# Batch 0 of a fused attention and two-block MLP kernel: strided heads first, mixing products as their inputs finish

## The chip, the cores and the metric

The kernel runs on one core of a Trainium2 chip. The metric is the time of one execution in microseconds (us): before the change the median of three runs is 950.33 us (949.88 to 951.0). A core has five engines that run at the same time and each take their instructions in a fixed order: TensorE (PE, matrix products; its weight loads are listed as PEld), VectorE (DVE), ScalarE (ACT), GpSimd (POOL) and SyncE (SP). Here SP only issues DMAs, and POOL mostly does.

## The reference

For 4 batches of 576 tokens, 8 heads of 64 compute attention, and two MLP blocks follow. Heads 0 to 3 see the last 32 tokens ("local"), heads 4 to 7 see every 32nd token ("strided").

```
scores = scale * np.matmul(q, k.transpose(0, 1, 3, 2))
mask_local = (rel >= 0) & (rel < stride)
mask_strided = (rel >= 0) & (pos[None, :] % stride == pos[:, None] % stride)
attn = softmax(where(mask_local if h < H // 2 else mask_strided, scores, -1e9))
x = (attn @ v), heads side by side            # [4, 576, 512]

h = xt @ U @ V                                # block 1: mixes tokens, U is 576x32, V is 32x576
u = x + h.transpose(0, 2, 1)
x = u + np.maximum(u @ w_ch1, 0.0) @ w_ch2    # 512 -> 2048 -> 512

mixed = np.real(fft(fft(x, axis=1), axis=2))  # block 2
u = x + mixed
un = (u - mu) / np.sqrt(var + 1e-06)
out = u + np.maximum(un @ w_ch1, 0.0) @ w_ch2
```

## The kernel before

The 2304 tokens lie in five chunks: four of 512 tokens, one for each batch (tile `ub0` to `ub3`), and one of 256 with what is left of all batches (`ur`). The MLP (`ffn`, L1109) goes chunk by chunk, in two halves of 1024 hidden units. A half is a first layer (L1140 to L1142, three matmuls for each product, since numbers are split into a high and a low 16-bit part), an eviction by ACT and DVE (L1146, L1147), and a second layer (L1172 to L1174). Of chunk 0 the first half's first layer is done for token tiles 0 and 1 first and then for 2 and 3, so it starts when two of the four tiles are ready.

Before the first MLP matmul stand the attention of batch 0 and the first weights. Attention is cut into nine units: `L00`, `L10`, `L01`, `L11` (local; head pair j, part u), `R` (the 64 left-over tokens, local) and `S00`, `S10`, `S01`, `S11` (strided). Each unit is a chain: scores on PE, a row maximum on DVE (L453), exponentials on ACT (L461), transposes on PE, a copy on ACT, the product with v on PE (L514, L557, L587), and the normalization on DVE (L466 to L473). Before the steps of a unit PE runs fillers (`warm`, L479), matmuls with no use; `WARM` says how many.

The strided units write their result in another token order to a tile `xs`. `unpermute` (L610) brings it into token order by a detour: SP stores `xs` to DRAM (`scr`) and loads it back into columns 256 to 511 of `ub0`. It is issued when the last of the four strided units is done. The token mixing takes two products: `mix_groups` (L623) splits each of six groups of the attention's output on ACT and DVE (L633, L634) and sums U's product into two PSUM banks `tb` (L637; groups 6, 8, 10 take `xs`, groups 0 and 2 `ub0`, group 4 `ur`); then `ts` is split (L672, L673), and V's product (L677) is added to `ub0` on DVE (L678), which needs the loaded-back columns. Then each tile is scaled, split, transposed on PE (L707) and copied (L711, L713), and is an operand of the MLP.

Weights come as 64-bit numbers in blocks of 128 rows (`raw`, 0.52 MB, four buffers; loads at L173). Of a block DVE makes 32-bit numbers (a cast at L147 and a shift at L150), and ACT sums the squares (L224). When eight blocks (a half) are through, one common scale follows (`w_scale`, L199), and each block is split (L166, L169). A buffer's next load waits for the shift.

Loads of batch 0 are issued by SP in the order of `LOADS` (L43; `r` left-over values, `l`, `s` queries and keys, `v`, `x` values, `m` the mixing matrices, `w` a weight block). Loads of batch 1 wait by `gate` (L390) for the first tile of `ub0` with V's product added.

Two lanes are written out by hand, side work (attention, later preparation) and weights. Until the first tiles are ready the string `STEPS` says which lane takes the next step; after that `TICKS`, one entry for each of 64 places inside chunks 0 and 1, and then the rates `RATES` by chunk, or `LATE` once the last FFT is done. PSUM banks come from pools with fixed counts (`bank`, L96).

## Time and profile before

| what | us |
|---|---|
| median of three runs | 950.33 (949.88 to 951.0) |
| the profiled execution | 948.61 |
| its span on the core | 946.8 |
| PE busy | 911.7 (96%) |
| DVE busy | 641.0 (68%) |
| ACT busy | 416.7 (44%) |

The profile is of one execution. Its span runs from the first to the last instruction; 1.81 us of its time lie around the span. Times in the rows are us from the start of the span. Busy time is the time in which an engine has an instruction running; for PE it does not tell useful matmuls from fillers, and a busy PE can be at half clock (the granted clock, 1.00 for 2.4 GHz and 0.50 for 1.2 GHz). A timeline row names a run of equal instructions; in brackets stands how long the engine stood idle just before it, and what ended that.

### The profile page before, as it was taken

What the parts mean: (1) busy time and instruction counts of PE and PEld (TensorE: products, weight loads), DVE (VectorE), ACT (ScalarE), POOL (GpSimd) and SP (SyncE); (2) the same over time, 40 slices, a digit from 0 to 9 for tenths busy, and PEclk for the clock granted to TensorE, in tenths of its full rate; (3) what the DMA queues carried; (4) which work ended last, traced back from release to release, by engine and by line L of the source; (5) the groups of instructions that cost most, each with busy time, mean ns of one, the idle gap of its engine ahead of it and who ended that gap; (6) DMA issues with size and microseconds to landing.
All of it is one profiled execution on the core that took longest, in us unless ns stands there. A gap on an engine that the chain in (4) does not pass through costs nothing.

```text
span 946.8 us, 15957 instructions
## 1 busy us (share of the span) xinstructions
PE 911.7 (96%) x6155; PEld 586.0 (62%) x6155; DVE 641.0 (68%) x1633; ACT 416.7 (44%) x996; POOL 47.9 (5%) x83
## 2 busy tenths in 40 slices
PE   8968999999999999999999989999999999999998
PEld 6747755555545664466456446555644588888897
DVE  2787967533343436642848966998699799865766
ACT  3865767423231433731537534342324264342433
POOL 1102100000000001100111300001000000000000
PEclk9958999999999999999999989999999999999999
DMA  9688761232201103501424400003010301212010
GB/s 316 219 268 263 261 238 50 63 101 96 66 20 27 40 12 115 174 1 33 120 91 158 120 14 2 0 7 83 1 39 7 79 7 34 41 52 34 2 46 24
DMA packets 64891, 78.62 MB, mean 83 GB/s; under 512 B 46512, under 2 KB 51760, under 8 KB 64816
## 3 DMA queue, kind: packets, MB, share of 16 engines
q1 hardware_dynamic: 59696, 44.49, 16.7%
q0 software_dynamic: 5120, 33.12, 10.4%
q8 instruction: 48, 0.79, 0.3%
q14 instruction: 27, 0.22, 0.1%
HBM read 60.16 MB, written 7.08 MB: 71 GB/s over the span
## 4 chain that ended last, share of the span: by engine, by line
PE 61%; DVE 17%; issue 9%; DMA 6%; ACT 4%; POOL 1%; SPq 1%; DVEq 0%; POOLq 0%; ACTq 0%
PE f L1140 7%; PE f L1141 7%; PE f L1142 7%; PE f L1172 7%; PE f L1173 7%; PE f L1174 7%; DMA raw<-in_w 3%; PE bk L1059 2%; PE bk L1057 2%; PE bk L1058 2%; DVE wslot L987 2%; DVE wslot L973 1%; DVE wslot L169 1%; DVE gl L981 1%; POOL raw L173 1%
## 5 line engine op out<-in xcount | busy, mean ns | idle before, releaser
L1140 PE MATMUL f<-ut,wslot 128*128 128x512 f16 (+1 forms) x480 | 170.7, 356 | 6.3 <-DVE gl L1147 5.6
L1141 PE MATMUL f<-ut,wslot 128*128 128x512 f16 (+1 forms) x480 | 169.9, 354 | 1.7 <-DMA ut<-lo 1.1
L1142 PE MATMUL f<-ut,wslot 128*128 128x512 f16 (+1 forms) x480 | 170.0, 354 | 0.0
L1172 PE MATMUL f<-wslot,gh 128*128 128x512 f16 x416 | 158.5, 381 | 0.8 <-DVE ub L1180 0.8
L1173 PE MATMUL f<-wslot,gh 128*128 128x512 f16 x416 | 158.2, 380 | 0.0
L1174 PE MATMUL f<-wslot,gl 128*128 128x512 f16 x416 | 158.2, 380 | 0.0
L1146 ACT ACTIVATE gh<-f 128x512 f16<-128x512 f32 (+1 forms) x120 | 64.3, 537 | 138.4 <-PE f L1142 137.9
L1147 DVE SCALAR_TENSOR_TENSOR gl<-f,gh 128x512 f16<-128x512 f32 (+1 forms) x120 | 73.8, 615 | 65.8 <-ACT gh L1146 64.6
L1141 PEld LDWEIGHTS <-wslot 128*128 128x128 f16 x480 | 47.6, 99 | 48.9 <-issue 11.2
L1140 PEld LDWEIGHTS <-wslot 128*128 128x128 f16 x480 | 47.8, 100 | 43.8 <-issue 4.8
L1142 PEld LDWEIGHTS <-wslot 128*128 128x128 f16 x480 | 47.5, 99 | 44.3 <-issue 2.1
L1174 PEld LDWEIGHTS <-gl 128*128 128x128 f16 x416 | 40.8, 98 | 49.2 <-issue 0.7
L1172 PEld LDWEIGHTS <-gh 128*128 128x128 f16 x416 | 41.4, 100 | 45.5 <-issue 0.5
L1173 PEld LDWEIGHTS <-gh 128*128 128x128 f16 x416 | 40.9, 98 | 44.8 <-issue 1.6
L1180 DVE SCALAR_TENSOR_TENSOR ub<-f,ivt,ub 128x512 f32<-128x512 f32 x48 | 35.6, 744 | 47.8 <-PE f L1174 47.7
L166 ACT ACTIVATE wslot<-wslot,wsc 128x512 f16<-128x512 f32 x64 | 46.0, 719 | 48.5 <-DVE wsc L230 23.3
L169 DVE SCALAR_TENSOR_TENSOR wslot<-wslot,wsc 128x512 f16<-128x512 f32 x64 | 47.8, 746 | 12.7 <-ACT wslot L166 11.9
L461 ACT ACTIVATE P<-bk,mx 108x64 f32<-108x64 f32 (+2 forms) x126 | 30.6, 331 | 45.8 <-DVE mx L456 36.5
L150 DVE SCALAR_TENSOR_TENSOR wslot<-raw,ztop 128x512 int32<-128x512 int32 x64 | 45.1, 713 | 3.6 <-ACT ztop L149 2.3
L224 ACT ACTIVATE wslot<-wslot 128x512 bf16<-128x512 f32 x64 | 40.1, 627 | 12.7 <-DVE wslot L150 7.8
L173 POOL DMA_DIRECT2D raw<-in_w x61 | 33.2, 544 | 246.1 <-DVE wslot L150 136.8
L453 DVE TENSOR_REDUCE mx<-bk 108x6 f32<-108x384 f32 (+4 forms) x44 | 19.8, 461 | 32.8 <-PE bk L496 19.2
(364 smaller groups left out, 1875.4 us busy)
## 6 DMA issues: line engine op xcount, KB each, us to landing
raw<-in_w POOLq DMA_DIRECT2D x61, 511.8 KB, 4.9
q<-in_ql SPq DMA_DIRECT2D x8, 576.0 KB
q<-in_qs SPq DMA_DIRECT2D x7, 594.0 KB
out<-ub SPq DMA_DIRECT2D x16, 256.0 KB
vl<-in_vl SPq DMA_DIRECT2D x8, 390.0 KB
vs<-in_vs SPq DMA_DIRECT2D x8, 390.0 KB
k<-in_kl SPq DMA_DIRECT2D x8, 320.0 KB
scr<-xs SPq DMA_DIRECT2D x8, 270.0 KB
```

What stands on the lines that cost most here:

```text
L150: V.scalar_tensor_tensor(out=i32(dst), in0=x, scalar=13, in1=zt, op0=ALU.logical_shift_right, op1=ALU.bitwise_or)
L166: A.activation(out=dst, in_=src, func=AF.Copy, scale=s)
L169: V.scalar_tensor_tensor(out=dst, in0=src, scalar=s, in1=hi, op0=ALU.mult, op1=ALU.subtract)
L173: (eng or G).dma_start(out=raw[:, 0:2047], in_=src[m].bitcast(U16)[:, 1:2048])
L1140: T.matmul(ps[:, 0:n], lhsT=wh, rhs=uh[:, k, cols], start=(k == 0), stop=False)
L1141: T.matmul(ps[:, 0:n], lhsT=wh, rhs=ul[:, k, cols], start=False, stop=False)
L1142: T.matmul(ps[:, 0:n], lhsT=wl, rhs=uh[:, k, cols], start=False, stop=(k == 3))
L1146: A.activation(out=gh[:, i, cols], in_=ps[:, 0:n], func=AF.Relu)
L1147: V.scalar_tensor_tensor(out=gl[:, i, cols], in0=ps[:, 0:n], scalar=0.0, in1=gh[:, i, cols], op0=ALU.max, op1=ALU.subtract)
L1172: T.matmul(ps, lhsT=ga, rhs=w[:, 0, :], start=(i == 0), stop=False)
L1173: T.matmul(ps, lhsT=ga, rhs=w[:, 1, :], start=False, stop=False)
L1174: T.matmul(ps, lhsT=gb, rhs=w[:, 0, :], start=False, stop=(i == HW - 1))
```

## The change

For batch 0 the strided units are put out first (`FIRST`), with their queries and keys in front in `qk` and their loads first in `LOADS`; `L01` and `L11` come after `R`. The mixing products no longer wait for all units: each of the six groups is put out when the units that it takes are done (`GNEED`), in the order of `MG0`, and the two `tb` banks are taken from the pool of four when the first group starts. The 24 fillers at the start become 28, the 75 others 57. `STEPS`, `TICKS`, `RATES` and `LATE` have new numbers. Batches 1 to 3 keep their order of units.

```diff
+GNEED = {0: ('L00', 'L10'), 2: ('L01', 'L11'), 4: ('R',), 6: ('S00', 'S10'), 8: ('S00', 'S10', 'S01', 'S11'), 10: ('S01', 'S11')}
...
-LOADS = ['r', 'l0', 'v0', 'v1', 'l1', 'm', 's0', 'w', 's1', 'x1', 'w', 'w', 'x0']
+LOADS = ['s0', 's1', 'x0', 'x1', 'm', 'l0', 'w', 'w', 'l1', 'v0', 'r', 'w', 'v1']
...
 MG = [[6, 0, 2], [8, 4, 10]]
...
-STEPS = 'ssssmmsssssmsssswswssswssssssswwwsswwwssssswswsswswsswssssswswswssssswswss'
...
+STEPS = 'ssmssssmsssmsssswssswsswsssssswsswwsssswwswswsswwssssssssswsssssssssswwswswwssw'
...
+FIRST = ['S00', 'S10', 'S01', 'S11', 'L00', 'L10', 'R', 'L01', 'L11']
+MG0 = [6, 8, 10, 0, 2, 4]
 ORDER = ['L00', 'L10', 'L01', 'L11', 'R', 'S00', 'S10', 'S01', 'S11']
...
             A.activation(out=ap, in_=late[0], func=AF.Copy)
...
     qk = []
-    QK = [(b, x, j) for b in range(NB) for x in "ls" for j in range(2)]
+    QK = [(b, x, j) for b in range(NB) for x in ("ls" if b else "sl") for j in range(2)]
...
     def qk_load():
         b, x, j = QK[len(qk)]
...
     def local_unit(b, j, u, q, k, v):
         Sb = bank()
-        if b == j == u == 0:
-            z = ones.bitcast(BF16)
-            warm(Sb[:, 0:256], WARM['i'], z[:, 0:128], z)
         nm = f'L{j}{u}'
         warm(Sb[:, 0:416], WARM[nm][0], idb, mL[1])
         n = LCOLS[u]
...
     def strided_unit(b, j, u, q, k, v, xs):
         Sb = bank()
+        if b == j == u == 0:
+            z = ones.bitcast(BF16)
+            warm(Sb[:, 0:256], WARM['i'], z[:, 0:128], z)
         nm = f'S{j}{u}'
         warm(Sb[:, 0:416], WARM[nm][0], idb, mL[1])
         msk = mS[u].rearrange("p (n w) -> p n w", n=1).to_broadcast([128, 3, 128]) if u else mS[u]
...
         xs = atp.tile([128, NT, 256], F32, tag="xs", bufs=1, name="xs")
         qk_upto(4 * b + 3)
         v = loaded if b == 0 else {n: VT[n[0]](b, int(n[1:] or 0)) for n in ("v0", "v1", "r", "x0", "x1")}
-        for u in ORDER:
+        l0, s0 = (4 * b, 4 * b + 2) if b else (2, 0)
+        for u in ORDER if b else FIRST:
             if u == "R":
-                yield u, rest_unit(b, qk[4 * b:4 * b + 2], v["r"]), xs
+                yield u, rest_unit(b, qk[l0:l0 + 2], v["r"]), xs
                 qk_upto(4 * b + (5 if b else 4))
                 continue
             j, i = int(u[1]), int(u[2])
             if u[0] == "L":
-                yield u, local_unit(b, j, i, *qk[4 * b + j], v[f"v{j}"]), xs
+                yield u, local_unit(b, j, i, *qk[l0 + j], v[f"v{j}"]), xs
             else:
-                yield u, strided_unit(b, j, i, *qk[4 * b + 2 + j], v[f"x{j}"], xs), xs
+                yield u, strided_unit(b, j, i, *qk[s0 + j], v[f"x{j}"], xs), xs
                 if i == 1 and b:
                     qk_upto(4 * b + 6 + j)
...
     def attention(b):
         live = []
         left = {u for u in ORDER if u[0] == "S"}
+        done = set()
+        rest = list(MG0) if b == 0 else []
         it = attn_units(b)
         more = True
         tb = None
...
                     live.append([u, nm])
                 except StopIteration:
                     more = False
-                    tb = [bank(), bank()]
-                    live.append([mix_groups(b, xs, tb, MG[0]), "M"])
+                    if b:
+                        tb = [bank(), bank()]
+                        live.append([mix_groups(b, xs, tb, MG[0]), "M"])
             for z in list(live):
                 try:
                     next(z[0])
                 except StopIteration:
                     live.remove(z)
                     left.discard(z[1])
+                    done.add(z[1])
+                    while rest and done.issuperset(GNEED[rest[0]]):
+                        if tb is None:
+                            tb = [pb.tile([128, 512], F32, tag="b", name="bk") for _ in range(2)]
+                        live.append([mix_groups(b, xs, tb, [rest.pop(0)]), "M"])
                     if z[1][0] == "S" and not left:
                         unpermute(b, xs)
                     continue
                 yield
-        yield from mix_groups(b, xs, tb, MG[1])
+        if b:
+            yield from mix_groups(b, xs, tb, MG[1])
         p0 = 32 * b
         ts = atp.tile([128, 512], F32R, tag="PT", bufs=PTB, name="ts")
         for x in (1, 0):
```

Three places show what moved. Line numbers in the rows of the change are 3 to 13 higher for the same instruction. First, DVE just ahead of the first MLP matmuls, before the change. `ut` with `xs`, `ub0` or `ur` is a mixing group's split (L634), `raw` and `wsc` rows are weight blocks, `ts` is the split before V's product.

```order
L150 SCALAR_TENSOR_TENSOR wslot_913<-raw_583,ztop1_87 128x512
L156 TENSOR_SCALAR wsc_97<-wsc_97 128x8
L634 TENSOR_TENSOR ut1_626<-xs_161,ut0_625 108x512
L158 TENSOR_SCALAR wsc_97<-wsc_97 128x8
L634 TENSOR_TENSOR ut1_626<-ub0_89,ut0_625 128x512
L147 CAST ztop0_86<-raw_611 128x512
L169 SCALAR_TENSOR_TENSOR wslot_396<-wslot_397,wsc_97,wslot_396 128x512
L634 TENSOR_TENSOR ut1_626<-xs_161,ut0_625 108x512
L634 TENSOR_TENSOR ut1_626<-ur_93,ut0_625 32x512
L169 SCALAR_TENSOR_TENSOR wslot_397<-wslot_412,wsc_97,wslot_397 128x512
L673 TENSOR_TENSOR ts_689<-bk_587,ts_689 32x256
L673 TENSOR_TENSOR ts_689<-bk_586,ts_689 32x256
```

Five of the six group splits stand here or just above, behind the last strided unit. With the change, DVE some 50 rows further up, where the last strided units end and the first local one begins (`mx` a row maximum, `rc` a reciprocal; L638 was L634):

```order
L638 TENSOR_TENSOR ut1_407<-xs_161,ut0_406 108x512
L470 RECIPROCAL rc_385<-rc_385 108x6
L150 CAST ztop0_86<-raw_147 128x512
L476 TENSOR_TENSOR xs_161<-bk_375,rc_385 108x3x128
L153 SCALAR_TENSOR_TENSOR wslot_432<-raw_147,ztop0_86 128x512
L638 TENSOR_TENSOR ut1_407<-xs_161,ut0_406 108x512
L456 TENSOR_REDUCE mx_425<-bk_414 128x4
L459 TENSOR_SCALAR mx_425<-mx_425 128x4
L638 TENSOR_TENSOR ut1_407<-xs_161,ut0_406 108x512
```

The three splits from `xs` have moved up here, between weight blocks and the local units. And with the change the rows ahead of the first MLP matmuls:

```order
L153 SCALAR_TENSOR_TENSOR wslot_886<-raw_577,ztop1_87 128x512
L159 TENSOR_SCALAR wsc_97<-wsc_97 128x8
L638 TENSOR_TENSOR ut1_407<-ub0_89,ut0_406 128x512
L161 TENSOR_SCALAR wsc_97<-wsc_97 128x8
L150 CAST ztop0_86<-raw_632 128x512
L150 CAST ztop1_87<-raw_638 128x512
L153 SCALAR_TENSOR_TENSOR wslot_920<-raw_632,ztop0_86 128x512
L172 SCALAR_TENSOR_TENSOR wslot_389<-wslot_390,wsc_97,wslot_389 128x512
L686 TENSOR_TENSOR ts_673<-bk_342,ts_673 32x256
L153 SCALAR_TENSOR_TENSOR wslot_948<-raw_638,ztop1_87 128x512
L172 SCALAR_TENSOR_TENSOR wslot_390<-wslot_432,wsc_97,wslot_390 128x512
L691 TENSOR_TENSOR ub0_89<-ub0_89,bk_682 128x512
```

One split (from `ub0`) and one half of `ts` are left at this place; the weight rows are as many as before. The second engine is SP, which issues DMAs in order: before the change, from the last loads of batch 0 to the first of batch 1 (`vs`, `vl` values, `scr` the detour).

```order
L427 DMA vs<-in_vs 128x780
L173 DMA raw<-in_w 128x2047 x2
L427 DMA vs<-in_vs 128x780
L421 DMA vl<-in_vl 32x2x65
L614 DMA scr_100<-xs 18x256 x2
L615 DMA scr_100<-xs 54x5x256 x2
L619 DMA ub_89<-scr_100 128x1x256 x2
L621 DMA ur<-scr_100 32x256
L619 DMA ub_89<-scr_100 128x1x256 x2
L621 DMA ur<-scr_100 32x256
L409 DMA q<-in_ql 128x1152
```

The small `vl` row is a load of batch 1 that went out ahead of the detour. With the change, the same stretch:

```order
L176 DMA raw<-in_w 128x2047
L423 DMA vl<-in_vl 96x1040
L424 DMA vl<-in_vl 32x2x65
L618 DMA scr_100<-xs 18x256
L619 DMA scr_100<-xs 54x5x256
L618 DMA scr_100<-xs 18x256
L619 DMA scr_100<-xs 54x5x256
L623 DMA ub_89<-scr_100 128x1x256 x2
L625 DMA ur<-scr_100 32x256
L424 DMA vl<-in_vl 32x2x65
L623 DMA ub_89<-scr_100 128x1x256 x2
L625 DMA ur<-scr_100 32x256
```

The detour follows the same loads, in four stores; the small `vl` load now stands between the two pairs of loads back into `ub0`, so that the second pair waits for what it waits for (the values of `L00` and `L01`, whose buffer it takes).

## Rows read from the trace of the kernel before

**Rows 1.** busy time of each engine over the whole page

```profile
PE 911.7 (96%) x6155; PEld 586.0 (62%) x6155; DVE 641.0 (68%) x1633; ACT 416.7 (44%) x996; POOL 47.9 (5%) x83
```

**Rows 2.** windows: busy us by engine (PE, PEld, DVE, ACT, POOL), clock, DMA share, GB/s

```profile
0.00:11.16 11.16, 8.74 (x46) 5.88 (x47) 0.17 (x1) 1.59 (x2) 2.96 (x9) 1.00 0.84 243
11.16:27.29 16.13, 16.05 (x145) 10.98 (x143) 9.26 (x34) 8.95 (x31) 0.00 (x0) 1.00 1.02 383
27.29:65.41 38.12, 28.38 (x205) 23.03 (x205) 30.35 (x80) 28.04 (x84) 6.03 (x11) 0.72 0.68 206
65.41:104.90 39.49, 36.16 (x333) 29.42 (x332) 31.47 (x94) 23.98 (x68) 6.44 (x12) 0.88 0.87 294
104.90:130.00 25.10, 24.56 (x177) 17.01 (x174) 20.48 (x51) 17.63 (x52) 4.96 (x9) 1.00 0.84 297
```

**Rows 3.** timeline of PE: start, us, line, what [idle before <-releaser]

```profile
10.03 1.10 PE L496 MATMUL bk<-k,q 128*128 128x96 f32 x8 [1.36 <-DMA q<-in_ql]
...
44.28 2.43 PE L557 MATMUL bk<-vs,PZ 128*108 128x65 f32 x12 [1.43 <-ACT PZ L547]
...
49.15 5.37 PE L637 MATMUL bk<-ut,US 108*128 108x256 f32 x16 [0.20 <-ACT ut L633]
55.44 1.22 PE L677 MATMUL bk<-ts,VS 128*128 128x512 f32 x2 [0.93 <-DVE ts L673]
62.38 0.61 PE L707 MATMUL bk<-idh,gh 128*128 128x128 f16 x4 [5.71 <-ACT gh L166]
...
65.52 0.74 PE L1140 MATMUL f<-ut,wslot 128*128 128x256 f16 x2
...
104.90 0.38 PE L1172 MATMUL f<-wslot,gh 128*128 128x512 f16 x1
```

**Rows 4.** timeline of DVE, the longest waits before the first FFN matmul

```profile
14.94 0.16 DVE L466 TENSOR_SCALAR rc<-bk 128x4 f32<-128x4 f32 x1 [3.01 <-PE bk L514]
...
18.73 0.56 DVE L453 TENSOR_REDUCE mx<-bk 128x4 f32<-128x384 f32 x1 [2.96 <-PE bk L496]
...
57.66 0.69 DVE L678 TENSOR_TENSOR ub<-ub,bk 128x512 f32<-128x512 f32 x1 [0.88 <-DMA ub<-scr]
59.00 0.69 DVE L678 TENSOR_TENSOR ub<-ub,bk 128x512 f32<-128x512 f32 x1 [0.66 <-DMA ub<-scr]
...
65.41 0.42 DVE L711 COPY ut<-bk 128x512 f16<-128x512 f16 x1
```

**Rows 5.** timeline of SP's DMA queue: the detour through DRAM

```profile
48.40 0.87 SPq L615 DMA_DIRECT2D scr<-xs  x2
53.45 1.24 SPq L619 DMA_DIRECT2D ub<-scr  x2
...
55.75 1.09 SPq L619 DMA_DIRECT2D ub<-scr  x2
```

**Rows 6.** groups of DVE instructions by form, 0 to 66 us

```profile
L150 DVE SCALAR_TENSOR_TENSOR wslot<-raw,ztop 128x512 int32<-128x512 int32 x12 | 8.1, 685 | 0.1
...
L634 DVE TENSOR_TENSOR ut<-xs,ut 108x512 fp32r<-108x512 f32 x3 | 2.1, 689 | 0.0
```

**Rows 7.** the weight loads of line L173, 0 to 140 us

```profile
DMA to landing us min/median/max: 3.7/5.1/9.7
```

**Rows 8.** timeline of PE, the same matmuls at two clocks

```profile
67.19 0.42 PE L1140 MATMUL f<-ut,wslot 128*128 128x256 f16 x1
67.41 0.42 PE L1141 MATMUL f<-ut,wslot 128*128 128x256 f16 x1
...
68.41 0.27 PE L1141 MATMUL f<-ut,wslot 128*128 128x256 f16 x1
68.51 0.27 PE L1142 MATMUL f<-ut,wslot 128*128 128x256 f16 x1
```

**Rows 9.** windows of the late part, columns as in rows 2

```profile
700.00:720.00 20.00, 18.71 (x87) 8.42 (x86) 20.00 (x54) 4.78 (x9) 0.00 (x0) 1.00 0.15 34
720.00:740.00 20.00, 20.00 (x94) 9.11 (x93) 19.70 (x73) 8.65 (x17) 0.00 (x0) 1.00 0.19 40
```

More of the change, by code (lines that the diff above doesn't have):

```diff
@@ L47 @@
 MG = [[6, 0, 2], [8, 4, 10]]
-TICKS = 'ws|wwsssww|wsswws|wwsw|wsws|swswwsw|w|swwswwssw|wsw|wsswwss|w|swsw|wwsww|wws|wwwsss|ssw|wwssws|wsssw|wswswsww|ss|ws|ssw|ssw|wss|swwsw|ww|swwss|wsw|wwsws|wws|ss|wwwwww|ww|www|wswwssw|wwsssss|wwww|w|ws|ww||w|ws|sssww|wswww|wwws|ws|wwss||sw|w|wwswwww||wssww|s|wwsw||ww||wwswwwws|sws|wwwwsww|ws|sws'
-STEPS = 'ssssmmsssssmsssswswssswssssssswwwsswwwssssswswsswswsswssssswswswssssswswss'
+TICKS = 'wws|wwwssw|swssw|sww|swssws|wwwsss||wwwss|wwws|wssswwwswww|s|wss|ww|sssw|swwsws|ww|sswswsww|wsswswws|wwsww|s|wwwwws|sws|ssww|ss|swsws|sw|wsswww|ssw|wwws|wsw|sw|wwws|s|wwww|sssws|swwwwwsswws|ww|w|s|wsww|www|ssw||wwsww|wsww|ws|wsww|wwswws||ss|wwsw|wwswww|s|wwwwss|w|ws|www|wswss|w|swswws|wwww|wwww|s|wwwsssw'
+STEPS = 'ssmssssmsssmsssswssswsswsssssswsswwsssswwswswsswwssssssssswsssssssssswwswswwssw'
 PTB = 2
-WARM = {'i': 24, 'L00': (1, 6, 3), 'L10': (5, 2, 2), 'L01': (6, 6, 1), 'L11': (5, 2, 4), 'R': (2, 6, 4), 'S00': (4, 5, 1), 'S10': (1, 3, 0), 'S01': (0, 3, 0), 'S11': (3, 3, 1)}
+WARM = {'i': 28, 'L00': (0, 3, 0), 'L10': (5, 0, 2), 'L01': (6, 3, 4), 'L11': (0, 6, 0), 'R': (1, 0, 6), 'S00': (0, 0, 6), 'S10': (6, 6, 0), 'S01': (3, 2, 1), 'S11': (0, 0, 3)}
+FIRST = ['S00', 'S10', 'S01', 'S11', 'L00', 'L10', 'R', 'L01', 'L11']
+MG0 = [6, 8, 10, 0, 2, 4]
 ORDER = ['L00', 'L10', 'L01', 'L11', 'R', 'S00', 'S10', 'S01', 'S11']
@@ L55 @@
 TP = (0, 1, 2, 3, 4, 5, 6, 7)
-LATE = [0.7999999999999999, 0.40000000000000013]
-RATES = [[3.5, 1.9], [3.5, 1.0], [3.0, 2.0], [4.25, 3.75], [1.5, 1.5], [1.05, 2.25], [1.0, 4.0], [2.0, 2.25], [4.25, 1.0], [1.9, 0.5]]
+LATE = [0.75, 0.7]
+RATES = [[2.5, 2.0], [2.5, 0.5], [2.0, 1.5], [5.0, 2.75], [1.5, 1.5], [1.05, 2.25], [1.0, 4.0], [3.45, 0.6999999999999998], [4.25, 2.0], [3.35, 2.0]]
 class Lane:
```

## The prediction

> **What bounds the kernel now.** I read the page's busy times first, then windows cut where the work changes, then the timelines of PE and DVE up to the first MLP matmuls, then SP's queue. PE is busy 96% of the span [rows 1], and from 104.90 us on it is busy nearly all the time with matmuls that the change does not alter. What can be won lies ahead of the first MLP matmul, which comes at 65.52 us [rows 3]. Until then PE works on attention and on fillers, and its mean clock in the last 38 us is 0.72 [rows 2]. So the question is what decides the 65.52 us.
>
> From the strided units' last product (44.28 us) to the MLP there are 21.2 us: mixing matmuls for 5.37 us, V's product at 55.44 us, a wait of 5.71 us for ACT's first split, and the transposes [rows 3]. DVE's timeline gives the reason for part of this: the additions to `ub0` stand 0.88 and 0.66 us for the detour through DRAM, stored at 48.40 us and fetched from 53.45 us on [rows 4, 5]. But DVE is the engine to count, for it works in order and does most of this. From its first row maximum at about 11.16 us to the copy at 65.41 us that lets the MLP go on, it is busy 9.26 + 30.35 = 39.6 of 54.25 us and idle 14.6 [rows 2, 4]. The idle time is 3.01 + 2.96 us in the first local units, which wait for PE [rows 4], about 0.9 us more before 27.29 us (16.13 - 9.26 = 6.87 in all), and 38.12 - 30.35 = 7.77 us later [rows 2]. The DMA engines are full in 11 to 27 us (share 1.02, 383 GB/s) and at 0.68 in 27 to 65 us [rows 2].
>
> **The change part by part.** *DVE's work.* In DVE's order I count 112 instructions from the first row maximum to the last one before the copy, 114 with the change: one split of a weight block less, one addition and its three small steps more, at most. With each form's mean (685 ns for a weight shift, 689 ns for a mixing split [rows 6], the rest from the same view) they sum to 46.1 and 46.35 us. The trace shows 39.6 us busy for the 46.1, since an instruction starts before the one ahead has ended: a factor of 0.86. So DVE has 39.6 x 46.35 / 46.1 = 39.8 us to do. No work disappears; only idle time can.
>
> *The start.* The first scores now need 1.35 MB ahead of them on SP's queue (masks, identity, `k` and `q` of `s0`), where it was 1.49 MB when they waited until 10.03 us [rows 3]. At 243 GB/s [rows 2] that is 0.6 us less, so the first row maximum comes at about 10.6 us.
>
> *The loads, which set a floor.* The 243 x 11.16 + 383 x 16.13 = 8.9 MB that batch 0 and four weight blocks need were in by 27.3 us [rows 2], and the change loads the same. The last four in the new order are `v0`, `r`, `w`, `v1`; behind `v0` come 1.07 MB or 2.8 us, so `v0` is there at 24.5 us. Two more weight blocks, asked for when the first two buffers come free, may take 1.05 MB or 2.7 us of the same engines: 27.2 us. I take 26. The first local normalization needs `v0` and its product (about 1 us): 27 us. By then DVE should have done the first 42 instructions, 16.4 of the 46.35 us or 14.1 us busy: from 10.6 us that ends at 24.7 us, so the units wait for loads there and 2.3 us of idle time take the place of the 6.9.
>
> The Trainium skill says the DMAs of SP, ACT and POOL run on the same 16 engines and interleave ("Trainium Kernel Development and Optimization", section Key Constraints), which speaks against bringing POOL's weight loads forward beside SP's queue. The trace agrees as far as it goes: with both queues loading, 11 to 27 us stays at 383 GB/s [rows 2]. By that rule `v0` would come at 27.2 us and the sum below would end 1.2 us later.
>
> *The rest.* From the first local normalization on, 72 instructions are left, 30.0 of the 46.35 us or 25.8 us busy: 27 + 25.8 = 52.8 us. Of the 7.77 us idle that this part had, the 1.54 us for the detour go: `xs` is complete 59 instructions (some 20 us of DVE's work by the same count) before the first addition, and from the last stores at 48.40 us to the second addition at 59.00 us [rows 4, 5] the detour took 10.6 us. Its second half now stands in SP's queue behind a load that waits for `L01`'s product; that product is 25 DVE instructions or some 10 us ahead of the addition of tile 2, and from the first fetch to the second addition it was 59.00 - 53.45 = 5.6 us [rows 4, 5], so this hides too. The two waits around `ts` (together 1.1 us) stay, since one half of `ts` is still at the end. Of the other 5.1 us, waits for single units at the end, I take half: local units now have weight blocks and mixing splits between them, but two of the four banks of one PSUM pool are taken by `tb` all that time, so none or all of it could remain. That gives 52.8 + 1.1 + 2.6 = 56.5 us for the first MLP matmul: **9.0 us earlier**. Ends: with `v0` at 24.5 us and no idle time 25 + 25.8 = 50.8 us (14.7 us earlier); with the last load, `v1`, decisive at 30 us and all small waits left 30 + 25.8 + 6.2 = 62.0 us (3.5 us earlier).
>
> *The weights.* In both orders DVE has shifted four blocks of the second matrix before the copy, and eight blocks lie between. A block's load takes 5.1 us in the middle, 9.7 at most [rows 7]; between a shift and the cast of the block that is loaded into its buffer lie 4.6 to 9 us of DVE's other work by the same count. At 5.1 us I cost it at nothing; without that cover it is the first rival.
>
> *Fillers.* 18 fewer among the units, 4 more at the start. PE was busy 16.05 of 16.13 us from 11 to 27 us [rows 2], fillers included, so fewer cannot hurt its queue; what they cost is the clock, a rival below.
>
> *After the start.* From 65.41 to 104.90 us the first layer's first half runs beside batch 1's units and the second matrix; 3.3 us of it PE is idle and the clock is 0.88 [rows 2]. With the change the stretch has the same instructions and the same loads, behind the same state, so it moves as a whole. The second matrix's scale stands 12 matmuls later (112 instead of 100 of 192), 1.3 us, inside the first layer. Entries of `TICKS` move a few steps: I take zero, with 2 us either way.
>
> *The late part.* Up to the third FFT, DVE's order in block 2 is the same. Then `LATE` brings up to 14 preparation instructions forward and pushes 9 pair sums back. At 0.41 to 0.69 us each [the last from rows 6] that is at most 7.7 us, in a stretch where DVE is busy 20.00 and 19.70 of 20 us. But with DVE at 19.70 PE was busy all 20.00 [rows 9], so a full DVE alone does not hold it up. I take zero; the ends are a gain of the 1.3 us that PE idles in the first of these windows and a loss of 7.7 us.
>
> **Sum.** 948.61 - 9.0 = 939.6 us for the profiled execution. The median of the runs is 1.72 us above that execution: **941.3 us**. Its own range, with 14.7 and 3.5 us earlier, is 935.6 to 946.8 us.
>
> **The rivals.** *Late weights.* If loads take 9.7 instead of 5.1 us [rows 7], because they now run beside batch 0's last loads, two rounds of four buffers cost 2 x 4.6 = 9.2 us on DVE, in order, and the MLP starts where it did: 950.5 us. For it: the full DMA engines until 27 us. Against: share 0.68 after that; the 7.9 MB of that stretch in 29 us would be 271 GB/s, below the 383 that were moved [rows 2].
>
> *The late part pays.* 7.7 us as above: 949.0 us. Against it stands the busy PE of [rows 9].
>
> *Slower: the low clock stays.* The same matmul follows the next after 0.22 us at 67.19 us and after 0.10 to 0.11 us at 68.41 us [rows 8]: 1.2 and 2.4 GHz. PE was at the low level after its thin stretch of mixing and got out 3 us into the MLP. The first half's first layer has 192 such matmuls. If PE, fed in drips by splits and by batch 1, stays at 1.2 GHz through it, that costs 192 x 0.106 = 20.4 us, of which the clock of 0.88 [rows 2] (a quarter of the time low) says a quarter was paid already: 15.5 more, 956.8 us. It decides from 103 further slow matmuls on ((9.0 + 1.9) / 0.106). For it: fewer fillers and waits for loads at 25 us. Against: the MLP's stream is the same and brought the clock back before. The Trainium skill states that the throttled state is the default and activity releases it ("TensorE: Matmul & The Clock Gate", section Part 1); the rows at 67 and 68 us agree.
>
> **How the numbers follow.** Forecast 0.78, late weights 0.07, the late part 0.07, low clock 0.08. About 0.2% (1.9 us) is what a measurement of this kernel can tell from no change. All of the forecast's range is faster by more; of the late part I count 0.02 as faster, the rest with late weights as the same: faster 0.80, same 0.12, slower 0.08. The range for 8 in 10 takes the forecast's own and reaches up towards the first two rivals: 935.5 to 949.5 us.
>
> **What would show it.** The first MLP matmul at 51 to 62 us, no DVE wait for the detour, `v0` and `v1` as the waits at 24 to 30 us, and the first second-layer matmul as much earlier as the first MLP matmul. The forecast is wrong if the MLP starts after 62 us, if second-layer work still starts near 105 us (then weights or batch 1's loads decide), or if the gain at 130 us is lost again by the end (then the new rates cost it).

## The result, and the profile after

The changed kernel takes 936.74 us in the median of six executions (932.16 to 941.28); the kernel before, run beside it, took 951.84 (949.88 to 956.96). The ratio is 0.984 (95% interval 0.981 to 0.987): faster by 15 us where 9 were forecast. The time lies in the forecast's range, but the sum behind it does not hold: its start was to give all of the gain and gives less than half of it.

Of the changed kernel there are two traces: the first is of the slowest of its six executions (941.28 us), the second, of the same program, is of a usual one (937.08). Of the kernel before, [rows 1 to 9] are of one of its fastest executions (948.61); a second trace, taken among the experiments, is of a usual one (952.48). They are called after, after (second), before and before (second). What counts is the usual against the usual, a difference of 15.4 us.

Busy times of the changed kernel, its first trace, against [rows 1]: PE is busy 7.5 us less, with 14 fillers gone and fewer matmuls at half clock. DVE has the same to do.

```profile
PE 904.2 (96%) x6141; PEld 579.2 (62%) x6141; DVE 640.8 (68%) x1633; ACT 416.5 (44%) x996; POOL 48.8 (5%) x83
```

Windows of the first trace, cut where those of [rows 2] are cut: at the first row maximum, the first local normalization (which the forecast's sum put at the end of the loads), the copy before the first MLP matmul, the point where PE has done the same 333 matmuls as in the fourth line there, and 130 us. Columns as there.

```profile
0.00:10.61 10.61, 6.95 (x46) 5.13 (x47) 0.17 (x1) 1.59 (x2) 2.97 (x9) 1.00 0.82 281
10.61:33.52 22.91, 22.15 (x179) 17.57 (x178) 14.96 (x42) 16.73 (x57) 1.08 (x2) 0.93 0.91 297
33.52:63.03 29.51, 18.60 (x157) 13.38 (x158) 24.99 (x72) 19.14 (x54) 5.38 (x10) 0.75 0.78 236
63.03:97.50 34.47, 33.25 (x333) 27.02 (x331) 30.57 (x91) 24.18 (x76) 6.13 (x11) 0.96 0.93 314
97.50:130.00 32.50, 32.25 (x228) 22.24 (x226) 25.59 (x59) 23.80 (x61) 4.85 (x9) 1.00 0.83 279
```

The second and third lines are the forecast's two parts of the start: 22.91 us instead of 16.4 to the first local normalization, with DVE busy 14.96 of them, and then 29.51 us with DVE busy 24.99.

PE's timeline of the first trace (start, us, line, what, [idle before <-releaser]), for [rows 3]:

```profile
9.45 1.12 PE L535 MATMUL bk<-k,q 128*108 128x54 f32 x10 [2.60 <-DMA q<-in_qs]
...
55.05 1.65 PE L690 MATMUL bk<-ts,VS 128*128 128x512 f32 x3 [3.44 <-DVE ts L686]
...
60.64 1.22 PE L720 MATMUL bk<-idh,gh 128*128 128x128 f16 x8 [3.94 <-ACT gh L169]
...
63.51 0.37 PE L1153 MATMUL f<-ut,wslot 128*128 128x256 f16 x1
...
96.05 0.38 PE L1185 MATMUL f<-wslot,gh 128*128 128x512 f16 x1
```

The first MLP matmul comes at 63.51 us, 2.0 us earlier than in [rows 3] and not 9.0. The first second-layer matmul comes at 96.05 us, 8.9 us earlier: the stretch between them fell from 39.4 to 32.5 us, which was forecast to move as a whole. Part of that is order, for 318 matmuls stand between the two points where 330 stood. Over the same 333 matmuls the stretch fell by 5.0 us, from 39.49 [rows 2] to 34.47 (the fourth window).

DVE's timeline of the first trace, for [rows 4], and SP's queue, for [rows 5]:

```profile
10.61 0.56 DVE L456 TENSOR_REDUCE mx<-bk 108x6 f32<-108x384 f32 x1 [9.61 <-PE bk L535]
...
15.38 0.56 DVE L456 TENSOR_REDUCE mx<-bk 108x6 f32<-108x384 f32 x1 [4.01 <-PE bk L535]
...
33.52 0.16 DVE L469 TENSOR_SCALAR rc<-bk 128x4 f32<-128x4 f32 x1 [0.17 <-PE bk L514]
...
52.85 0.46 DVE L150 CAST ztop<-raw 128x512 f16<-128x512 bf16 x1 [3.02 <-DMA raw<-in_w]
...
63.03 0.90 DVE L724 COPY ut<-bk 128x512 f16<-128x512 f16 x2
```

```profile
31.09 0.92 SPq L619 DMA_DIRECT2D scr<-xs  x1
...
35.65 1.42 SPq L623 DMA_DIRECT2D ub<-scr  x2
...
43.20 1.10 SPq L623 DMA_DIRECT2D ub<-scr  x2
```

The 3.01 and 2.96 us of the local units have become 4.01 us for the second strided unit's scores (2.75 us in the second trace, whose row follows). No addition waits for the detour any more, whose halves are fetched at 35.65 and 43.20 us. In its place a cast of a weight block waits 3.02 us at 52.85 us.

```profile
14.32 0.56 DVE L456 TENSOR_REDUCE mx<-bk 108x6 f32<-108x384 f32 x1 [2.75 <-PE bk L535]
```

The same points in all four traces, in us from the start of the span (an eviction is one of line L1147, L1160 in the changed kernel; they come in the same order in both kernels, so the 25th is the same work):

| | before | before (second) | after (second) | after | second less second |
|---|---|---|---|---|---|
| first row maximum | 11.16 | 13.50 | 10.81 | 10.61 | -2.7 |
| first MLP matmul | 65.52 | 68.31 | 61.84 | 63.51 | -6.5 |
| 25th eviction | 205.54 | 205.03 | 195.57 | 199.36 | -9.5 |
| 53rd | 381.56 | 381.08 | 369.98 | 373.78 | -11.1 |
| 57th | 411.24 | 416.40 | 399.72 | 403.84 | -16.7 |
| 117th | 724.14 | 728.42 | 713.73 | 717.88 | -14.7 |
| span | 946.8 | 950.7 | 935.3 | 939.5 | -15.4 |

So, read from point to point, 6.5 of the 15.4 us are gained up to the first MLP matmul (2.7 of them up to the first row maximum), 3.0 up to the 25th eviction, 1.6 up to the 53rd, and 5.6 us at one place between the 53rd and the 57th, of which 2.0 are given back later; the end gives 0.7. These are places and not yet causes: two executions of one program differ by 1.7 to 2.8 us at the first MLP matmul and by 0.5 to 3.8 us at the 25th eviction. That one place is also where the two executions of the kernel before part: the second is 0.5 us ahead of the first at the 53rd eviction and 5.2 us behind at the 57th.

There the second layer's first weights are loaded. First the second trace of before: ACT's timeline, PE's, SP's, POOL's, and windows with the columns of [rows 2].

```profile
396.56 0.72 ACT L166 ACTIVATE hi<-ub,sct 128x512 f16<-128x512 f32 x1 [3.84 <-DMA ut<-hi]
398.67 0.72 ACT L166 ACTIVATE hi<-ub,sct 128x512 f16<-128x512 f32 x1 [1.40 <-DMA ut<-hi]
```

```profile
402.30 0.38 PE L1172 MATMUL f<-wslot,gh 128*128 128x512 f16 x1 [4.78 <-DVE ub L1180]
```

```profile
386.98 1.23 SPq L715 DMA_TRANSPOSE ut<-lo  x1
388.31 2.55 SPq L715 DMA_TRANSPOSE ut<-hi  x2
390.96 1.52 SPq L715 DMA_TRANSPOSE ut<-lo  x1
```

```profile
383.94 0.54 POOL L173 DMA_DIRECT2D raw<-in_w  x1 [8.43 <-DVE wslot L150]
...
388.84 0.54 POOL L173 DMA_DIRECT2D raw<-in_w  x1 [2.02 <-DVE ea L777]
390.35 0.55 POOL L173 DMA_DIRECT2D raw<-in_w  x1 [0.97 <-DMA raw<-in_w]
```

```profile
380.00:400.00 20.00, 17.47 (x81) 7.70 (x79) 12.61 (x39) 14.23 (x33) 3.23 (x6) 1.00 0.73 184
400.00:420.00 20.00, 17.70 (x101) 10.27 (x101) 8.46 (x17) 5.25 (x11) 0.00 (x0) 0.91 0.00 1
```

SP issues DMA transposes of `hi` and `lo` from 386.98 to 390.96 us; POOL issues five weight blocks from 383.94 to 390.35 us, three ahead of the transposes and two among them. ACT may write `hi` again only when the transposes have read it, and stands 3.84 and 1.40 us for them; PE then stands 4.78 us for what follows, and its granted clock is 0.50 from 403 to 406 us (0.91 in the mean of the second window). In the first trace of before the blocks and the transposes are mixed in the same way, yet the same waits of ACT are shorter and PE stands only 0.8 us:

```profile
394.68 0.72 ACT L166 ACTIVATE hi<-ub,sct 128x512 f16<-128x512 f32 x1 [1.84 <-DMA ut<-hi]
396.60 0.72 ACT L166 ACTIVATE hi<-ub,sct 128x512 f16<-128x512 f32 x1 [1.19 <-DMA ut<-hi]
```

In the changed kernel (second trace; ACT, SP, POOL, windows) the transposes are issued before the next weight loads, ACT does not wait, and PE is busy all 20 us:

```profile
382.90 1.32 ACT L169 ACTIVATE hi<-ub,sct 128x512 f16<-128x512 f32 x2
```

```profile
377.65 1.24 SPq L728 DMA_TRANSPOSE ut<-lo  x1
378.99 2.50 SPq L728 DMA_TRANSPOSE ut<-hi  x2
381.58 1.22 SPq L728 DMA_TRANSPOSE ut<-lo  x1
```

```profile
381.99 1.21 POOL L176 DMA_DIRECT2D raw<-in_w  x2 [8.44 <-DVE sct L159]
388.13 1.14 POOL L176 DMA_DIRECT2D raw<-in_w  x2 [4.94 <-DVE wslot L153]
```

```profile
380.00:400.00 20.00, 20.00 (x105) 10.04 (x103) 12.64 (x39) 11.83 (x26) 3.23 (x6) 1.00 0.56 178
```

The Trainium skill says that a DMA engine takes turns between the queues' rings, a packet at a time ("DMA: Bandwidth & Descriptors", section Queues, rings and completion order). The second trace of before is in line with it: from 380 to 402 us SP's queue moved 0.52 MB in 2176 packets and POOL's 3.15 MB in 483, so a transpose's small packet may stand behind one 27 times its size. No run here takes the two apart.

### The profile page after: what moved, and what is told of

The parts are those of the page before. It is cut to its first block, busy times and chain, and to the rows that moved or that the text cites. A ratio compares the mean times of both kernels' runs of the same rounds, so it can differ in the third digit from the quotient of the medians.

```text
span 939.5 us, 15926 instructions
## 1 busy us (share of the span) xinstructions
PE 904.2 (96%) x6141; PEld 579.2 (62%) x6141; DVE 640.8 (68%) x1633; ACT 416.5 (44%) x996; POOL 48.8 (5%) x83
## 4 chain that ended last, share of the span: by engine, by line
PE 62%; DVE 20%; issue 7%; DMA 5%; ACT 4%; POOL 1%; SPq 1%; DVEq 0%; POOLq 0%; ACTq 0%
PE f L1153 7%; PE f L1154 7%; PE f L1155 7%; PE f L1185 6%; PE f L1187 6%; PE f L1186 6%; PE bk L1072 3%; PE bk L1071 3%; PE bk L1070 3%; DMA raw<-in_w 2%; DVE wslot L1000 2%; DVE wslot L172 2%; DVE gl L1160 1%; DVE wslot L986 1%; PE bk L535 1%
## 5 line engine op out<-in xcount | busy, mean ns | idle before, releaser
L1160 DVE SCALAR_TENSOR_TENSOR gl<-f,gh 128x512 f16<-128x512 f32 (+1 forms) x120 | 73.8, 615 | 56.0 <-ACT gh L1159 55.2
L464 ACT ACTIVATE P<-bk,mx 108x64 f32<-108x64 f32 (+2 forms) x126 | 31.1, 330 | 39.6 <-DVE mx L459 36.7
```

The lines of the kernel that those rows point to most:

```text
L1160: V.scalar_tensor_tensor(out=gl[:, i, cols], in0=ps[:, 0:n], scalar=0.0, in1=gh[:, i, cols], op0=ALU.max, op1=ALU.subtract)
```

## The experiments

Times are medians; ratios are against the kernel before, run beside them on the same chip, with their 95% interval. Its medians there are 951.99 us (16 executions, 949.27 to 957.42) for the first four runs, 952.99 (23, 949.0 to 956.91) for the two with a fifth buffer and the two with one part alone, and 952.26 (19, 945.82 to 960.26) for the last four.

**The change once more.** No edit.

> The changed kernel once more, for its spread and a second trace. Theory 'start' (all of the gain is made before the first MLP matmul, and the first trace caught an execution with an unusually late start at 63.5 us): this trace, if its execution is faster than 941 us, starts the MLP correspondingly earlier (at 56 to 58 us for 934 us). Rival 'after the start' (the gain is made between the first MLP matmul and the first second-layer matmul): the start stays within 62 to 65 us and that stretch takes 33 to 35 us where it took 39.4 us before.

936.87 us, ratio 0.984 (0.981 to 0.987). Its trace is the "after (second)" above: with the clock at 1.00 in the first 20 us the MLP starts 1.7 us earlier than in the first trace, where it was 0.91, and the 25th eviction comes 3.8 us earlier. One program thus varies by about 4 us up to its 25th eviction. The rival "after the start" is the nearer one: the MLP starts only 1.7 us earlier for 4.2 us less time, at 61.84 us, and the stretch is 32.97 us.

**The tables.** The change with the old `TICKS`, the kernel before with the new, and the change with the old rates:

```diff
-TICKS = 'wws|wwwssw|swssw|...'     # change, new
+TICKS = 'ws|wwsssww|wsswws|...'    # change, old (and the reverse in before)
-LATE = [0.75, 0.7]                 # third run, with RATES
+LATE = [0.7999999999999999, 0.40000000000000013]
```

> The change with the old TICKS. If the new TICKS shortened the stretch from the first MLP matmul to the first second-layer matmul (39.4 us before, 32.5 us in the first trace after), it is back at 38 to 40 us here and the kernel is about 6 us slower than the change. If the stretch is shorter because the order before it left the loads and the clock in a better state, it stays at 32 to 35 us and the time is within 2 us of the change.

> The kernel before with only the new TICKS. If the new TICKS are what shortens the stretch after the first MLP matmul, about 6 us faster than before. If they only fit the new order of batch 0, within 2 us of before or slower.

> The change with the old RATES and LATE. The first trace after gains 1.0 us between 700 us and the end. If that is the new rates: 1 us slower than the change, and nothing else moves. If the late part pays for preparation brought forward: faster than the change by up to 7.7 us. If neither: the same within 1 us.

Old `TICKS` in the change: 935.88 us, ratio 0.983 (0.980 to 0.986), no difference from the change; the stretch to the first second-layer matmul is 34.78 us. New `TICKS` in before: 947.02 us, ratio 0.994 (0.992 to 0.996), a gain of 5 us. So the table is worth something only where the rest is old. That stretch is 40.28 us in before with new `TICKS`, no shorter, but 366 matmuls stand in it and not 330, so between tables it cannot be compared. The eighth eviction can: from the first MLP matmul to it are 26.2 and 25.2 us in before, 23.0 with new `TICKS`, 21.4 and 21.9 in the change, 22.0 with old `TICKS`. One reason for the gain of the table is thus in the stretch after the start. In before a cast of a weight block stands there for its load, in DVE's order ahead of batch 1's row maxima; first trace, second trace, the change (first trace), and before with new `TICKS`:

```profile
82.33 0.46 DVE L147 CAST ztop<-raw 128x512 f16<-128x512 bf16 x1 [3.02 <-DMA raw<-in_w]
```

```profile
84.89 0.46 DVE L147 CAST ztop<-raw 128x512 f16<-128x512 bf16 x1 [2.45 <-DMA raw<-in_w]
```

```profile
78.89 0.46 DVE L150 CAST ztop<-raw 128x512 f16<-128x512 bf16 x1 [1.34 <-DMA raw<-in_w]
```

```profile
80.44 0.55 DVE L147 CAST ztop<-raw 128x512 f16<-128x512 bf16 x1 [0.54 <-DMA raw<-in_w]
```

Both the change and the new `TICKS` make the wait shorter (in the change with old `TICKS` it is gone), so together they win it once. The other reason is at the transposes: before with new `TICKS` is 3.1 us ahead of before (second) at the 53rd eviction and 9.7 us at the 57th. There, too, either table is enough. Old rates in the change: 938.43 us, ratio 0.986 (0.983 to 0.989), 1.6 us more than the change, with overlapping intervals. PE's idle time from 700 to 930 us is 6.9 and 6.5 us in before, 5.9 in both traces of the change and 6.2 with the old rates: the late part gives 0.7 to 1.1 us, of which the old rates take back a third to a half. The rates also explain the 1.6 us between the 25th and the 53rd eviction: that distance is 176.0 to 176.7 us in all seven traces with old rates and 173.1 to 174.4 in all seven with new ones. The change with old rates has 1.0 us of that back by the 57th (28.7 us from the 53rd, against 29.7 in after (second)). In before with new `TICKS`, and in the change with old rates, the blocks near 380 us are loaded ahead of the transposes (issued from 375.12 and 369.15 us on, the transposes from 383.92 and 377.97), and ACT waits 3.31 and 2.38 us once; PE does not stand for it. With the new rates they come behind.

**A fifth raw buffer**, in before and in the change:

```diff
-RAWS = 4
+RAWS = 5
```

> The kernel before with one edit: five buffers for raw weight blocks instead of four, so that every block can be asked for one block earlier. Theory A (the second part of the gain is the weight block that came late: DVE stood 3.02 us for it at 82.33 us in the trace of before, batch 1's scores came late behind it, and PE fell to half its clock from 83.7 to 92 us): no cast of a weight block waits over 1 us between 70 and 90 us, the stretch from the first MLP matmul to the first second-layer matmul falls from 39.4 to about 34 us, the first MLP matmul stays near 65 us, and the time falls by 4 to 6 us, to 946 to 948. Theory B (the stretch is shorter with the change because PE and the units of batch 1 reach it in another order, not because of that block): the stretch stays at 38 to 40 us and the time at 950 to 953.

> The changed kernel with five raw buffers instead of four. In the changed kernel a cast of a weight block waits 2 to 3 us at 46 to 53 us, ahead of the first MLP matmul, and the stretch after it has already lost its waits. Theory A (weight blocks are waited for wherever four buffers run out): that wait goes, the first MLP matmul comes 1 to 3 us earlier than the 59.3 to 63.5 us of the four traces, the stretch stays near 33 us, time 934 to 936. Theory B (the wait at 46 to 53 us is beside the path, which goes over the mixing and ts): 936 to 938, as the changed kernel.

In before: 952.6 us, ratio 1.000 (0.999 to 1.002). The time speaks for theory B, the trace for A in the stretch: no cast waits over 0.54 us, and the stretch is 34.4 us, with 330 matmuls in it as before. The start is later than A had it, 70.06 us and not 65. What was won there was lost at the transposes. Window of the stretch, and PE behind the transposes:

```profile
70.06:104.49 34.43, 33.82 (x332) 27.45 (x331) 30.17 (x90) 23.28 (x66) 6.83 (x13) 0.94 0.98 329
```

```profile
403.70 0.58 PE L1172 MATMUL f<-wslot,gh 128*128 128x512 f16 x1 [9.59 <-DVE ub L1180]
```

At the 53rd eviction this kernel is 3.4 us ahead of before (second), at the 57th 2.3 behind: ACT stood 8.68 and 3.49 us for the transposes. In the change: 935.47 us, ratio 0.983 (0.980 to 0.985), not distinct from the change. No cast waits ahead of the MLP any more, and from 40 us to it DVE idles 1.07 us and not 3.34, but it has 2 us more of other work there, and the MLP starts at 63.19 us. From the first row maximum, late here at 12.37 us, it is 50.8 us, against 51.0 and 52.9 in the change. The first second-layer matmul comes late, at 101.67 us, but 366 matmuls stand ahead of it; the eighth eviction comes 21.2 us after the MLP's start, as in the change. The time is theory B's: taking that wait away moves nothing that the times show.

**One part of the change alone.** Before with groups put out singly, and the change with groups at the end:

```diff
+            while rest and done.issuperset(GNEED[rest[0]]):     # into before; tb taken here
+                live.append([mix_groups(b, xs, tb, [rest.pop(0)]), "M"])
```

```diff
-            while rest and done.issuperset(GNEED[rest[0]]):     # in the change
+            while rest and done.issuperset(FIRST):
```

> The kernel before with one part of the change: batch 0's mixing groups are put out one by one as their units finish, while units, loads, fillers and tables stay as before. Theory A (the order of the units is what brings the start forward: with local units first the strided products end only at 44.28 us, and four of the six groups need them): the first MLP matmul moves by less than 2 us from 65.5, time 949 to 953. Theory B (the groups' early output alone fills the waits at the end of the start): first MLP matmul at 60 to 63 us, time 946 to 948.

> The changed kernel without one part: mixing groups are put out only when all nine units are done, while units, loads, fillers and tables are those of the change. Theory A (the early groups matter: six groups' splits of 0.69 us and their matmuls, 5.4 us on PE in the kernel before, come back behind the last unit): the first MLP matmul 3 to 5 us later than in the change, time 940 to 942. Theory B (the order of units and loads brings it all): within 1 us of the change, 936 to 938.

Singly with the old order: 958.73 us, ratio 1.006 (1.004 to 1.008), slower by nearly 6 us, which neither theory had. PE and DVE of that run:

```profile
51.20 2.43 PE L559 MATMUL bk<-vs,PZ 128*108 128x65 f32 x12 [0.73 <-ACT PZ L549]
...
73.69 1.22 PE L718 MATMUL bk<-idh,gh 128*128 128x128 f16 x8 [11.96 <-ACT gh L168]
...
76.56 0.37 PE L1151 MATMUL f<-ut,wslot 128*128 128x256 f16 x1
```

```profile
65.09 0.69 DVE L689 TENSOR_TENSOR ub<-ub,bk 128x512 f32<-128x512 f32 x1 [2.35 <-DMA ub<-scr]
...
71.34 0.69 DVE L689 TENSOR_TENSOR ub<-ub,bk 128x512 f32<-128x512 f32 x1 [2.80 <-DMA ub<-scr]
```

The last strided product ends at 53.6 us instead of 46.7, and the MLP starts at 76.56 us. The two `tb` banks are taken from the pool of four when the first local units are done, ahead of all strided units, which then share what is left; that this is the cause is read from the order, not tried. The detour starts later by as much, and the additions stand 2.35, 1.35 and 2.80 us for it. So early groups, written this way, lose without the strided units in front. Groups at the end in the change: 940.71 us, ratio 0.987 (0.985 to 0.990), 3.8 us more than the change, which ran on another chip; the intervals of the ratios overlap. The time is theory A's, the place is not: its MLP starts at 62.52 us, within the change's traces, 51.7 us behind its first row maximum. So in this trace what the start wins came without the early groups. This run loses later: PE stands 0.9 us for batch 1's mixing and then 2.08 us for exponentials (the rows are the start and this wait), and the 25th eviction comes 5.5 us later than in after (second) and 1.7 later than in after. How the early groups prevent that is not shown.

```profile
62.52 0.37 PE L1153 MATMUL f<-ut,wslot 128*128 128x256 f16 x1
```

```profile
169.64 0.31 PE L505 MATMUL bk<-ident,P 128*96 128x128 f32 x1 [2.08 <-ACT P L464]
```

**The detour.** Before, with no store to wait for:

```diff
-            S.dma_start(out=ub[b][:, g, 256:512], in_=sv_[f, 4 * k:4 * k + 4])
+            S.dma_start(out=ub[b][:, g, 256:512], in_=ql[b, 0][:, 256 * g:256 * g + 256] if b == 0 else ...)
```

> The kernel before, in which columns 256 to 511 of batch 0's attention result are loaded from the input q in place of the DRAM buffer that the strided results were stored to (the same number of loads and bytes at the same place in the queue; the part of the computation that is changed is that batch 0's strided attention results don't enter the sum with the mixing product). So the additions to ub0 wait for no store. Theory A (the 0.88 and 0.66 us that DVE stood for the detour are on the path): no wait of DVE for it, the first MLP matmul 1.5 us earlier, time 1 to 2 us under before. Theory B (behind these waits stand others, ACT's split after the addition and the transposes, that end no earlier, or batch 1 takes it back): time within 1 us of before.

952.83 us, ratio 1.001 (0.999 to 1.004). The waits are gone (the additions run as one row at 62.01 us), but from the first row maximum to the first MLP matmul it is 54.5 us, as in before (54.4 and 54.8). The 1.54 us were not on the path: theory B.

**A second trace of before**, no edit:

> The kernel before once more, for a second trace of it: the profiled execution of the first was 948.61 us where the median of its executions in all calls is 952 to 953. Theory A: the missing 3 to 4 us lie in the start and in the stretch behind it (first MLP matmul at 66 to 69 us, a weight block waited for again for 2 us or more at 75 to 90 us). Theory B: they lie behind the start, at 380 to 420 us, where in two variants ACT stood 5.5 to 9.6 us for DMA transposes that ran beside the loads of the second layer's weights, and in the first trace of before it did not: PE idle over 5 us in 380 to 420 us, the start as before within 1 us.

952.48 us in its one execution. Theory A's signs are there: the start is later by 2.8 us (first row maximum at 13.50 us, MLP at 68.31) and a block is waited for again, 2.45 us. But by the 25th eviction the late start is made up, and the place is theory B's, with PE idle for 4.83 us from 380 to 420 us where B said over 5. What stays is the 5.6 us at the transposes.

**Fillers.** The change without those of the first two strided units, and with the old table:

```diff
-'S00': (0, 0, 6), 'S10': (6, 6, 0)
+'S00': (0, 0, 0), 'S10': (0, 0, 0)
```

> The changed kernel without the 18 filler matmuls ahead of the steps of the first two strided units (28 fillers ahead of the first scores stay). Theory A (PE's queue holds the strided chain up: six fillers at half clock, 0.34 us each, and the transposes of S00 stand ahead of S10's scores, which come at 14.13 us, and DVE waits 4.01 us for them): the second row maximum at 13 to 14 us instead of 15.38, the first local normalization 1 to 3 us earlier than 33.52, first MLP matmul at 58 to 62 us, time 935 to 936.5. Theory B (the fillers keep the clock: in the traces with a clock of 1.00 in the first 20 us the MLP started at 59 to 62 us, in those with 0.83 to 0.91 at 63.2 to 63.5): clock in the first 20 us at 0.85 or less, the MLP at 63 to 65 us, time 937 to 940.

> The changed kernel with the fillers of the kernel before: 24 ahead of the first scores instead of 28, 79 among the units instead of 56. Theory A (fillers cost nothing while PE waits anyway, and their table is without effect): 936 to 938, start at 59 to 64 us. Theory B (23 more fillers of 0.18 to 0.34 us, 4 to 6 us of PE's time, half of them where PE is the engine waited for): first MLP matmul 2 to 3 us later, time 939 to 941.

Without: 941.41 us, ratio 0.992 (0.989 to 0.995), 4.5 us more than the change. DVE's and PE's timeline and the first 20 us of this run, and the same window of after (second):

```profile
11.66 0.56 DVE L456 TENSOR_REDUCE mx<-bk 108x6 f32<-108x384 f32 x1 [10.66 <-PE bk L535]
16.11 0.56 DVE L456 TENSOR_REDUCE mx<-bk 108x6 f32<-108x384 f32 x1 [3.68 <-PE bk L535]
```

```profile
13.10 1.26 PE L543 MATMUL bk<-ident,gh 108*128 108x108 f32 x3 [1.47 <-ACT gh L464]
14.15 1.92 PE L535 MATMUL bk<-k,q 128*108 128x54 f32 x10
```

```profile
0.00:20.00 20.00, 14.87 (x76) 11.82 (x77) 2.00 (x8) 5.15 (x16) 2.96 (x9) 0.74 0.90 341
```

```profile
0.00:20.00 20.00, 17.21 (x124) 13.13 (x124) 4.41 (x15) 6.95 (x21) 2.96 (x9) 1.00 0.91 344
```

The clock falls to 0.74, the second row maximum comes no earlier, and the MLP starts at 66.97 us: theory B, whose own bounds of 65 us and 940 us are passed. With these fillers the traces of this order have 0.83 (with the fifth buffer) to 1.00. S10's scores come at 14.15 us without the fillers and at 14.13 and 13.21 us with them: they stand in PE's order behind S00's transposes (L543), which wait for exponentials. With the old table, 18 more among the units (the counts in that expectation are off: they are 75 and 57): 936.57 us, ratio 0.984 (0.981 to 0.987). The time is theory A's; the MLP starts at 65.20 us, later than A had it, and by the 25th eviction that is made up (199.31 us).

## Why the prediction was right and where it was wrong

- *DVE's work* (39.6 to 39.8 us): right, 14.96 + 24.99 = 39.95 us.
- *The start* (first row maximum at 10.6): right, 10.61 and 10.81. But the 11.16 us of before was a good execution; its second trace has 13.50. Over all traces it is 8.8 to 12.4 us in the eight with the changed order and 11.2 to 14.7 in the six with the old one. The means lie 1.8 us apart where 0.6 were forecast, but the ranges overlap.
- *The loads, which set a floor*: this step failed. The first local normalization was put at 27 us, with 2.3 us of idle DVE for `v0`, and came at 33.52, with 7.95 us idle (32.46 and 6.69 us in the second trace). DVE did not wait for a load but for PE, 4.01 us for S10's scores (2.75 in the second trace, with the clock at 1.00) and 1.04, 0.99 and 0.63 us in the next. The strided units are one chain at their start, as the local ones were: the step let the waits of the local units go without putting those of the strided ones in their place. Taking the fillers ahead of S10's scores away did not bring them forward, though the clock fell with it.
- *The rest*: the size is right, 24.99 + 4.52 = 29.51 us against 25.8 + 3.7. Its make-up is not: the 1.54 us of the detour were never on the path, and a weight block took 3.02 us.
- *The weights hidden*: they are not, but with a fifth buffer the wait goes and the time stays. *Fillers at nothing*: right for the table as a whole, and wrong as a rule, since without those of the first two units the clock fell to 0.74 and the kernel took 4.5 us more.
- So from the first row maximum to the MLP it is 51.0 and 52.9 us in the change, against 54.4 and 54.8 before: 1.5 to 3.8 us less, where the sum had 8.4. The MLP starts at 59.3, 61.8, 63.4 and 63.5 us in the four traces with this order of the start (the change twice, with old `TICKS`, with old rates), and not at 56.5: two of the four lie beyond the 62 us that the forecast named as its own failure.
- *After the start, moves as a whole*: this failed in the other direction. In before PE lost 3.3 us idle and 4.7 us by its clock in this stretch [rows 2]; the change's first trace has 1.2 and 1.4. The rows of before had the waits, but the forecast took it that they would move along. They hung on a weight block that was 3.02 and 2.45 us late in before and 1.34 and 1.49 us in the change; a fifth buffer in before takes that wait away, and the distance to the eighth eviction falls from 25 or 26 to 21 us, as in the change.
- *The late part at nothing*: 0.7 to 1.1 us, within its ends. That the new rates would gain 1.6 us between the 25th and the 53rd eviction was not in the sum.
- *Not seen at all*: the 5.6 us at the transposes. The profiled execution of before was one in which PE stood only 0.8 us there, and only the 1.72 us between that execution and the median hinted that such a place might exist. That the order of transposes and weight loads is the cause rests on comparing traces: PE stood 4.8, 5.5, 6.5 and 9.6 us in four traces with loads and transposes mixed, 0.8 in the fifth, and at most 0.2 in the nine where the loads stand ahead or behind. The fifth shows that the order alone does not decide it, and no run moved these loads alone: the cause stays open.
- The rivals: late weights and the late part did not come, nor did the low clock; the clock in the stretch rose to 0.96.
- So that the time fell into the range is in good part luck: the start gave less than the sum had for it, and places that stood at nothing in the sum gave the rest and more.

## What to carry to other kernels

When several units are put in front, their own chain replaces the one that was there: count its waits (here 2.8 to 4 us for the second unit's scores) before a wait is booked as gone. A wait on a busy engine is worth what the next point on PE's row gains, so read the distance between two points of the work and not the wait: the detour's 1.5 us were worth nothing, a block's 3 us some 3 to 5. And compare a kernel's profiled execution with its median first: here it was 1.7 us faster than the first three runs' median, and a second trace showed a stall of 4.8 us that the first one hid.

## What was not expected of the hardware

DMA transposes beside weight loads: in the change (second) DVE's split that waits for the last `lo` to be read starts 4.9 us after the last issue (381.58 to 386.48), in before (second), with loads among them, 9.9 us after it (390.96 to 400.83). In before, with the same loads among them, the same split starts 5.9 us after it (391.44 to 397.35): such loads can hold transposes up, and need not. One program's start varies by itself: without any edit the first MLP matmul came at 65.5 and 68.3 us in before and at 61.8 and 63.5 us in the change, with the clock at 1.00 or 0.91 in the first 20 us; and starts from 63.5 to 67.0 us ended up at the same 25th eviction (199.0 to 199.4 us in after, the change with old fillers and with few). What evens them out stays open.
